# An attention loop regrouped: rounds of two score tiles, P·V in five bursts a head pair instead of nine

## The chip, the core and the metric

The kernel runs on one core of a Trainium2 chip. The metric is the device time of one execution in microseconds. The engines named below are TensorE (PE, its weight loads listed apart as PEld), VectorE (DVE), ScalarE (ACT), GpSimd (POOL) and the queue that issues the DMAs (SP).

## The reference

Attention over 2 batches and 8 heads, 1152 positions, head dimension 64, with the queries averaged in pairs (576 query rows), then a gated sum of four two-layer experts on the 1152 x 512 result, all in float32:

```python
q_pool = q.reshape(B, H, S // 2, 2, D).mean(axis=3)
scores = scale * np.matmul(q_pool, k.transpose(0, 1, 3, 2))
attn = np.exp(scores - np.max(scores, axis=-1, keepdims=True))
attn = attn / (np.sum(attn, axis=-1, keepdims=True) + 1e-09)
x = np.matmul(attn, v)            # then to (1152, 512)
for e in range(E):
    h = np.maximum(x @ w1[e], 0.0)
    out += p[:, e:e + 1] * (h @ w2[e])
```

## The kernel before

The attention stage goes over 8 pairs of heads (`n`). A pair has nine score tiles `i` of 128 query rows by 1152 keys: tiles 0 to 7 alternate between the two heads, tile 8 holds the last 64 rows of both. The 72 tiles are numbered through as `g = 9n + i`. A tile goes through these steps:

- `S_chunk` (L240): six matmuls (nine for tile 8) of 384 columns into the score tile `spt`, three banks of PSUM. The pool `ps_s` has one such buffer.
- `neg_scores` (L253): one DVE instruction takes all of `spt`, scales it, finds the row minimum `mn` and writes `sx`, of which there are three (`g % 3`).
- `exps` (L258): one ACT activation over `sx` in place, with the row sums into `sums`.
- `T_chunk` (L263): three transposes of 128 x 128 into a PSUM tile `pt`, three chunks a tile; the copy of chunk 1 into `aT` is on DVE, those of chunks 0 and 2 are on ACT.
- `PV_part` (L284): P·V from `aT` and `vn` into `po`, group 0 for tiles 0 to 3 (256 columns) and group 1 for tiles 4 to 8 (320 columns). Each of nine key blocks `kt` is a matmul for either head, 64 output columns wide, and the trace lists it as two instructions: four `L293` a key block. What is issued in one go is called a burst here.
- `diag_sums`, `spread_sums`, `finish` (L299 to L333): the reciprocal of the row sums (DVE, then POOL into `dg`), spread by four small matmuls into `rb`, and the division when a group is complete.

In between `prep_q` and `prep_k` transpose the next pair's queries and keys (three and five pieces), which POOL has split before (`split_pool`, `add_q`); SP moves their halves into place (`stack_k` into `kab`, the DMAs at L210 into `q2`).

The pool `ps_t` has four PSUM buffers under one tag: every `T_chunk`, every piece of `prep_q` and `prep_k` and every `spread_sums` takes one, in the order of the program, and the buffer comes free when its copy out has read it. `ps_o` has one buffer for `po`. Nothing is reordered: the kernel is built with a manual schedule, and each engine runs its instructions in the order in which the program emits them.

One round of the loop handles one tile, in the order of `ORDER`: `T0 prep T1 exp T2 P S bx`. So PE transposes tile g, prepares a piece for the next pair, does a burst of two or so key blocks, and makes the scores of tile g + 2; ACT's exponential of tile g + 1 stands between the copies of tile g. The matmuls of the first expert chunk are cut into 32 units: `fill(2)` puts two into each of the last two rounds, `fill(4)` four ahead of the last `spread_sums` and `PV_part`, and `fill(32)` the rest behind them. The expert stage follows (L461 on).

Of the kernel before, what the change touches and what calls it, by code (L numbers as in the profile page):

```python
# [17 lines left out]
def attention_moe_kernel(ctx, tc, q, k, v, probs, w1, w2, out):  # L18
    nc = tc.nc
# [3 lines left out]
    P = 128  # L23
# [89 lines left out]
    with ExitStack() as actx:  # L113
# [62 lines left out]
        def split_pool(dst, src):  # L176
            for h in range(2):
                split_rows(dst[:, h], src[:, h])
# [179 lines left out]
        for c in range(3):  # L358
            S_chunk(1, c)
        neg_scores(1)  # L360
        prep_q(0, 2)
        load_q(1)
        load_kv(kn, k, 1)
        add_q(nc.gpsimd)
# [5 lines left out]
        PVCUT = {0: (1, -1, 0, 3), 1: (1, -1, 3, 5), 2: (1, -1, 5, 7), 3: (1, -1, 7, 9),  # L370
                 4: (0, 0, 0, 2), 5: (0, 0, 2, 4), 6: (0, 0, 4, 6), 7: (0, 0, 6, 8), 8: (0, 0, 8, 9)}
        STAGES = {0: [(stack_k, 0, 0)], 1: [(stack_k, 0, 1)], 3: [(diag_sums, 0, 0)], 8: [(diag_sums, 0, 1)]}
        SPREAD = {6: (0, 0), 1: (-1, 1)}
        PREP = [None, ("q", 0), ("k", 0), ("k", 1), ("k", 2), ("q", 2), ("k", 3), ("k", 4), None]

        def pv_part(g):
            n, i = divmod(g, 9)
            grp, dn, k0, k1 = PVCUT[i]
            if 0 <= n + dn < NP:
                PV_part(n + dn, grp, k0, k1)  # L380

# [16 lines left out]
        ORDER = 'T0 prep T1 exp T2 P S bx'.split()  # L398
# [11 lines left out]
        for g in range(NTL):  # L410
            n, i = divmod(g, 9)
            if i == 4 and 0 < n and n + 1 < NP:
                load_kv(vn[(n + 1) % 2], v, n + 1)
            if i == (6 if n else 7) and n + 2 < NP:
                add_q(nc.gpsimd)
            if i == 0 and 0 < n and n + 1 < NP:
                split_pool(khl, kn)
            if i == 2 and 0 < n and n + 2 < NP:
                load_q(n + 2)
                load_kv(kn, k, n + 2)  # L420
            for step in ORDER:
                if step[0] == "T":
                    T_chunk(g, int(step[1]))
                elif step == "prep" and n + 1 < NP:
                    what = PREP[i]
                    if what:
                        (prep_q if what[0] == "q" else prep_k)(n + 1, what[1])
                elif step == "exp" and g + 1 < NTL:
                    exps(g + 1)
                elif step == "P":  # L430
                    pv_part(g)
                    if i in SPREAD and n + SPREAD[i][0] >= 0:
                        spread_sums(n + SPREAD[i][0], SPREAD[i][1])
                elif step == "S" and g + 2 < NTL:
                    for c in range(3):
                        S_chunk(g + 2, c)
                    neg_scores(g + 2)
                elif step == "bx":
                    for fn, dn, *args in STAGES.get(i, []):
                        fn(n + dn, *args)  # L440
            if (n, i) == (NP - 2, 0):
                load_weights(0)
            if (n, i) == (NP - 2, 7):
                load_weights(1)
                for kt in range(4):
                    split_weights(wslot[0], raw_piece(0, kt), kt)
            if (n, i) == (NP - 1, 2):
                load_weights(2)
            if (n, i) == (NP - 1, 7):
                for kt in range(4):  # L450
                    split_weights(wslot[1], raw_piece(1, kt), kt)
                load_weights(3)
            if g >= NTL - 2:
                fill(2)
# [101 lines left out]
```

## Time and profile before

| | us |
|---|---|
| median of 3 runs | 687.33 (686.88 to 687.66) |
| the profiled execution | 686.85 |
| its span in the trace | 685.1 |
| attention loop from the scores of tile 2 to the last `spread_sums` | 14.29 to 280.14 |
| PE busy in the span | 677.1 (99%) |

The execution's own time is 1.75 us above its span. A busy PE is not a PE at its peak: matmul ends in the trace are modelled and overlap, so the starts of the weight loads are what the order of the work is read from.

### The profile page before, as it was taken

Reading aid. Unit: us, or ns where it says so; the run is one execution under the profiler, and the core shown is the slowest. Engines: PE = TensorE matmul, PEld = TensorE weight load, DVE = VectorE, ACT = ScalarE, POOL = GpSimd, SP = SyncE. Lnnn points to the kernel's source line nnn. Section 1 sums busy time; section 2 is a strip of 40 time slices with the busy share of each in tenths; the row PEclk is TensorE's granted clock in tenths of the full one; section 3 lists DMA queues with packets and bytes.
Section 4 is the critical chain, followed back from the end, with each engine's and each line's share of the span. In section 5 each row is a group of like instructions: output and inputs, shape, how many; then the busy total and the mean of one; then the engine's idle time right before and its main releaser. Section 6 shows DMA issues by size and latency. Waiting matters only on the chain.

```text
span 685.1 us, 9897 instructions
## 1 busy us (share of the span) xinstructions
PE 677.1 (99%) x3986; PEld 576.2 (84%) x3986; DVE 248.1 (36%) x453; ACT 239.0 (35%) x473; POOL 201.9 (29%) x243
## 2 busy tenths in 40 slices
PE   7999999999999999999999999999999999999998
PEld 6777777777777777799989898989898989898987
DVE  5756565655656555321212121212121212121211
ACT  5867676767676666321111010101010202020200
POOL 4232323232323515392260080350170430310000
PEclk9999999999999999999999999999999999999999
DMA  7726262626252841031030030030040000001012
GB/s 241 168 52 184 54 181 59 179 61 174 64 172 54 235 131 51 12 123 61 1 124 1 0 95 30 29 94 1 0 124 1 32 30 1 0 1 32 15 43 52
DMA packets 26446, 50.75 MB, mean 74 GB/s; under 512 B 2464, under 2 KB 9888, under 8 KB 26400
## 3 DMA queue, kind: packets, MB, share of 16 engines
q1 hardware_dynamic: 26400, 50.12, 26.1%
q8 instruction: 32, 0.52, 0.3%
q14 instruction: 14, 0.11, 0.0%
HBM read 30.97 MB, written 2.36 MB: 49 GB/s over the span
## 4 chain that ended last, share of the span: by engine, by line
PE 91%; POOL 2%; ACT 2%; DVE 2%; issue 1%; DMA 1%; SPq 0%; POOLq 0%; DVEq 0%; ACTq 0%
PE p L504 29%; PE p L93 27%; PE spt L251 11%; PE po L293 11%; PE pt L268 9%; PE p1t L93 2%; ACT sx L260 2%; DVE sx L254 2%; PE pk L224 1%; PE pr L316 1%; DMA kn<-in_k_dram 1%; POOL q2all L102 1%; PE pq L198 0%; POOL q2all L99 0%; POOL dg L305 0%
## 5 line engine op out<-in xcount | busy, mean ns | idle before, releaser
L93 PE MATMUL p<-xh,wslot 128*128 128x384 f32 x640 | 166.7, 339 | 0.0
L254 DVE TENSOR_SCALAR_CACHE_REDUCE sx<-spt 128x1152 f32<-128x1152 f32 x72 | 97.7, 1357 | 101.8 <-PE spt L251 101.3
L93 PEld LDWEIGHTS p<-xh,wslot 128*128 128x128 f32 x640 | 116.7, 188 | 0.4
L93 PE MATMUL p<-xl,wslot 128*128 128x384 f32 x320 | 108.3, 338 | 0.0
L260 ACT ACTIVATE sx<-sx,mn 128x1152 f32<-128x1152 f32 x72 | 90.5, 1257 | 28.6 <-DVE sx L254 24.9
L268 PE MATMUL pt<-ident,sx 128*128 128x128 f32 x648 | 91.2, 275 | 0.9 <-ACT sx L260 0.4
L280 ACT ACTIVATE aT<-pt 128x384 f32<-128x384 f32 x144 | 69.6, 483 | 50.2 <-PE pt L268 49.9
L251 PEld LDWEIGHTS spt<-k,q2all 128*128 128x128 f32 x384 | 64.0, 188 | 27.4 <-DVE aT L278 9.7
L251 PE MATMUL spt<-k,q2all 128*128 128x384 f32 x384 | 84.8, 355 | 0.8 <-DVE sx L254 0.4
L293 PE MATMUL po<-aT,vn 128*64 128x320 f32 (+1 forms) x576 | 85.0, 418 | 0.0
L268 PEld LDWEIGHTS pt<-ident,sx 128*128 128x128 f32 x648 | 74.2, 141 | 6.5 <-ACT sx L260 4.5
L95 ACT ACTIVATE hb<-p 128x384 fp32r<-128x384 f32 x48 | 23.6, 491 | 160.0 <-PE p L93 160.0
L504 PE MATMUL p<-wslot,hb 128*128 128x512 f32 (+1 forms) x348 | 75.8, 375 | 0.0
L504 PEld LDWEIGHTS p<-wslot,hb 128*128 128x128 f32 x348 | 62.2, 188 | 11.7
L509 DVE SCALAR_TENSOR_TENSOR acc<-p,pw,acc 128x512 f32<-128x512 f32 (+1 forms) x28 | 20.5, 732 | 124.1 <-PE p L504 124.1
L333 POOL TENSOR_TENSOR xl<-xs,xh 128x256 fp32r<-128x256 f32 (+2 forms) x20 | 13.4, 677 | 165.0 <-ACT xh L332 165.0
L93 PEld LDWEIGHTS p<-xl,wslot 128*128 128x128 f32 x320 | 60.0, 188 | 0.4
L95 ACT ACTIVATE k<-p 128x384 fp32r<-128x384 f32 x30 | 14.7, 492 | 130.6 <-PE p L93 130.6
L293 PEld LDWEIGHTS po<-aT,vn 128*64 128x64 f32 x576 | 35.3, 136 | 27.1 <-issue 11.4
L99 POOL TENSOR_SCALAR wslot<-stg 128x512 fp32r<-128x512 f32 x12 | 7.5, 624 | 162.3 <-PE p L93 84.7
L96 DVE SCALAR_TENSOR_TENSOR hb<-p,hb 128x384 fp32r<-128x384 f32 x48 | 26.7, 557 | 76.7 <-ACT hb L95 76.7
L504 PE MATMUL p<-wslot,k 128*128 128x512 f32 x168 | 51.9, 390 | 0.0
(102 smaller groups left out, 770.1 us busy)
## 6 DMA issues: line engine op xcount, KB each, us to landing
kab<-k SPq DMA_DIRECT2D x32, 288.0 KB, 4.7
q2all<-q2all SPq DMA_DIRECT2D x28, 256.0 KB, 4.9
vn<-in_v_dram SPq DMA_DIRECT2D x8, 576.0 KB, 6.9
kn<-in_moe_w_dram SPq DMA_DIRECT2D x8, 512.0 KB, 3.7
qn<-in_moe_w_dram SPq DMA_DIRECT2D x8, 512.0 KB, 3.7
stg<-in_moe_w_dram SPq DMA_DIRECT2D x8, 512.0 KB, 3.5
qs<-in_moe_w_dram SPq DMA_DIRECT2D x8, 512.0 KB, 3.6
qn<-in_q_dram SPq DMA_DIRECT2D x7, 576.0 KB, 6.3
```

The lines of the kernel that those rows point to most:

```text
L93: nc.tensor.matmul(pt, w[:, a, kt, fs], x[:, kt, cols], start=(j == 0), stop=(j == last))
L95: nc.scalar.activation(hh[ft], pt, AF.Relu)
L96: nc.vector.scalar_tensor_tensor(hl[ft], pt, 0.0, hh[ft].bitcast(F32), ALU.max, ALU.subtract)
L251: nc.tensor.matmul(spt[g][:, c, :NC], w, x, start=(j == 0), stop=(j == len(ops) - 1))
L254: nc.vector.tensor_scalar(sx[g % 3].rearrange("p (c x) -> p c x", c=3), spt.pop(g)[:, :, :NC], -INV, None, ALU.mult, ALU.min, accum_out=mn ...
L260: nc.scalar.activation(sx[g % 3], sx[g % 3], AF.Exp, bias=mn[g % 3], scale=-1.0, accum_out=sums[n % 2][:, i:i + 1])
L268: nc.tensor.transpose(pt[:, j, :], sx[g % 3][:, kt * P:(kt + 1) * P], ident)
L280: nc.scalar.activation(dst, src, AF.Copy)
L293: nc.tensor.matmul(po[h * HALF:(h + 1) * HALF, :w], vn[n % 2][:, h, kt, :], aT[grp][:, h, kt, :], start=(kt == 0), stop=(kt == KT - 1))
L333: nc.gpsimd.tensor_tensor(xl[:, hp, c], x[:, s0:s0 + w], xh[:, hp, c].bitcast(F32), ALU.subtract)
L504: nc.tensor.matmul(pc, h[ft][:, ts_], where[e, 2, ft // 4][:, a, ft % 4, c0:c1], start=(m == 0), stop=(m == len(ops) - 1))
L509: nc.vector.scalar_tensor_tensor(ac, pc, pw[:, tt, e:e + 1], ac, ALU.mult, ALU.add)
```

## The change

The loop goes in rounds of two tiles (`i` = 0, 2, 4, 6) and a last round of one (`i` = 8). A round emits: the transposes of tile g, the exponential of tile g + 2, the transposes of tile g + 1, up to two pieces of preparation for the next pair, the scores of tile g + 3, one burst of P·V, the exponential of tile g + 3, and the scores of tile g + 4. The round of tile 8 has its transposes, a burst and the scores of tile g + 3. P·V goes in five bursts of 5 and 4 key blocks (group 1 of the pair before) and 3, 3 and 3 (group 0), where there were nine. `stack_k` and `split_pool` move to the round of tile 8 of the pair before, the pieces of preparation to rounds 0, 2, 4 and 6, the loads and `diag_sums` by one to three tiles; the scores of tile 2 and the exponential of tile 1 move ahead of the loop. In the last pair `fill(4)` stands where scores are missing.

```diff
@@ -358,26 +358,37 @@
         for c in range(3):
             S_chunk(1, c)
         neg_scores(1)
+        exps(1)
         prep_q(0, 2)
+        for c in range(3):
+            S_chunk(2, c)
+        neg_scores(2)
         load_q(1)
         load_kv(kn, k, 1)
+        for h in range(2):
+            stack_k(0, h)
         add_q(nc.gpsimd)
         split_pool(khl, kn)
         load_kv(vn[1], v, 1)
         load_q(2)
         load_kv(kn, k, 2)
 
-        PVCUT = {0: (1, -1, 0, 3), 1: (1, -1, 3, 5), 2: (1, -1, 5, 7), 3: (1, -1, 7, 9),
-                 4: (0, 0, 0, 2), 5: (0, 0, 2, 4), 6: (0, 0, 4, 6), 7: (0, 0, 6, 8), 8: (0, 0, 8, 9)}
-        STAGES = {0: [(stack_k, 0, 0)], 1: [(stack_k, 0, 1)], 3: [(diag_sums, 0, 0)], 8: [(diag_sums, 0, 1)]}
-        SPREAD = {6: (0, 0), 1: (-1, 1)}
-        PREP = [None, ("q", 0), ("k", 0), ("k", 1), ("k", 2), ("q", 2), ("k", 3), ("k", 4), None]
-
-        def pv_part(g):
-            n, i = divmod(g, 9)
+        PVCUT = {0: (1, -1, 0, 5), 2: (1, -1, 5, 9), 4: (0, 0, 0, 3), 6: (0, 0, 3, 6), 8: (0, 0, 6, 9)}
+        SPREAD = {6: (0, 0), 0: (-1, 1)}
+        PREP = {0: [("q", 0), ("q", 2)], 2: [("k", 0), ("k", 1)], 4: [("k", 2), ("k", 3)], 6: [("k", 4)]}
+
+        def pv_part(n, i):
             grp, dn, k0, k1 = PVCUT[i]
             if 0 <= n + dn < NP:
                 PV_part(n + dn, grp, k0, k1)
+            if i in SPREAD and n + SPREAD[i][0] >= 0:
+                spread_sums(n + SPREAD[i][0], SPREAD[i][1])
+
+        def scores(g):
+            if g < NTL:
+                for c in range(3):
+                    S_chunk(g, c)
+                neg_scores(g)
 
         for hh in range(2):
             nc.sync.dma_start(
@@ -395,7 +406,6 @@
                     nc.vector.tensor_copy(pw[sl, 5 * b:5 * b + 4, :], pr[sl, 9 * b + a:9 * b + 8:2, :])
                 nc.vector.tensor_copy(pw[sl, 4, :], pr[sl, 9 * a + 8, :])
 
-        ORDER = 'T0 prep T1 exp T2 P S bx'.split()
         tail = []
         units = [(ft, kt) for ft in range(NFT) for kt in range(NKT)]
 
@@ -407,51 +417,62 @@
                         tail.append(ps_t.tile([P, NC], F32, tag="t", name="p1t"))
                     mm1_ft(0, 0, ft, tail[-1], kt)
 
-        for g in range(NTL):
-            n, i = divmod(g, 9)
-            if i == 4 and 0 < n and n + 1 < NP:
-                load_kv(vn[(n + 1) % 2], v, n + 1)
-            if i == (6 if n else 7) and n + 2 < NP:
-                add_q(nc.gpsimd)
-            if i == 0 and 0 < n and n + 1 < NP:
-                split_pool(khl, kn)
+        for n, i in [(n, i) for n in range(NP) for i in range(0, 9, 2)]:
+            g = 9 * n + i
+            last = n == NP - 1
             if i == 2 and 0 < n and n + 2 < NP:
                 load_q(n + 2)
                 load_kv(kn, k, n + 2)
-            for step in ORDER:
-                if step[0] == "T":
-                    T_chunk(g, int(step[1]))
-                elif step == "prep" and n + 1 < NP:
-                    what = PREP[i]
-                    if what:
-                        (prep_q if what[0] == "q" else prep_k)(n + 1, what[1])
-                elif step == "exp" and g + 1 < NTL:
-                    exps(g + 1)
-                elif step == "P":
-                    pv_part(g)
-                    if i in SPREAD and n + SPREAD[i][0] >= 0:
-                        spread_sums(n + SPREAD[i][0], SPREAD[i][1])
-                elif step == "S" and g + 2 < NTL:
-                    for c in range(3):
-                        S_chunk(g + 2, c)
-                    neg_scores(g + 2)
-                elif step == "bx":
-                    for fn, dn, *args in STAGES.get(i, []):
-                        fn(n + dn, *args)
+            if i == 4:
+                if 0 < n and n + 1 < NP:
+                    load_kv(vn[(n + 1) % 2], v, n + 1)
+                diag_sums(n, 0)
+            if i == 6 and n + 2 < NP:
+                add_q(nc.gpsimd)
+            if i == 8:
+                diag_sums(n, 1)
+                if n + 1 < NP:
+                    for h in range(2):
+                        stack_k(n + 1, h)
+                if n + 2 < NP:
+                    split_pool(khl, kn)
+            for c in range(3):
+                T_chunk(g, c)
+            if g + 2 < NTL:
+                exps(g + 2)
+            if i < 8:
+                for c in range(3):
+                    T_chunk(g + 1, c)
+            if not last:
+                for kind, c in PREP.get(i, []):
+                    (prep_q if kind == "q" else prep_k)(n + 1, c)
+            if i < 8:
+                scores(g + 3)
+                if last and i == 6:
+                    fill(4)
+                pv_part(n, i)
+                if g + 3 < NTL:
+                    exps(g + 3)
+                scores(g + 4)
+                if last and i == 6:
+                    fill(4)
+            else:
+                if last:
+                    fill(4)
+                pv_part(n, i)
+                scores(g + 3)
             if (n, i) == (NP - 2, 0):
                 load_weights(0)
-            if (n, i) == (NP - 2, 7):
+            if (n, i) == (NP - 2, 6):
                 load_weights(1)
                 for kt in range(4):
                     split_weights(wslot[0], raw_piece(0, kt), kt)
             if (n, i) == (NP - 1, 2):
                 load_weights(2)
-            if (n, i) == (NP - 1, 7):
+            if (n, i) == (NP - 1, 6):
                 for kt in range(4):
                     split_weights(wslot[1], raw_piece(1, kt), kt)
                 load_weights(3)
-            if g >= NTL - 2:
-                fill(2)
         fill(4)
         spread_sums(NP - 1, 1)
         PV_part(NP - 1, 1, 0, KT)
```

## Rows read from the trace of the kernel before

**Rows 1.** The head of the page: the span, and busy time, share of the span and instructions of each engine.

```profile
span 685.1 us, 9897 instructions
...
PE 677.1 (99%) x3986; PEld 576.2 (84%) x3986; DVE 248.1 (36%) x453; ACT 239.0 (35%) x473; POOL 201.9 (29%) x243
```

**Rows 2.** Busy time of each engine by stage: the stretch in us, its length, busy time and (x) instructions of PE, PEld, DVE, ACT and POOL, granted clock of PE as a share of 2.4 GHz, DMA share and GB/s. The edges are starts of the scores of tile 2: of pair 0, pair 1 and pair 7, then the last `spread_sums`.

```profile
...
14.29:45.13 30.84, 30.21 (x214) 23.61 (x214) 20.65 (x40) 23.83 (x47) 8.84 (x11) 1.00 0.58 140
45.13:248.82 203.69, 203.37 (x1448) 153.72 (x1446) 121.54 (x228) 141.75 (x279) 68.09 (x87) 1.00 0.49 131
248.82:280.14 31.32, 31.08 (x211) 24.05 (x209) 15.38 (x29) 18.96 (x38) 12.83 (x18) 1.00 0.12 39
280.14:685.10 404.96, 401.64 (x2056) 365.53 (x2056) 82.59 (x143) 47.49 (x98) 106.44 (x114) 1.00 0.12 38
```

**Rows 3.** Weight loads of PE in order of time through one round of a middle pair: start, length, line, names, shape and count, and in brackets the idle time before the load and what ended it. Scores, transposes of chunk 0, a piece of `prep_k`, transposes of chunks 1 and 2, a burst, the next scores.

```profile
...
151.38 1.01 PEld L251 LDWEIGHTS spt<-k,q2all 128*128 128x128 f32 x6 [0.49 <-DVE aT L278]
152.38 0.42 PEld L268 LDWEIGHTS pt<-ident,sx 128*128 128x128 f32 x3
152.77 0.42 PEld L224 LDWEIGHTS pk<-identr,khl 128*128 128x128 f32 x4
153.14 0.64 PEld L268 LDWEIGHTS pt<-ident,sx 128*128 128x128 f32 x6
153.95 0.74 PEld L293 LDWEIGHTS po<-aT,vn 128*64 128x64 f32 x8 [0.17 <-issue]
155.18 1.00 PEld L251 LDWEIGHTS spt<-k,q2all 128*128 128x128 f32 x6 [0.49 <-issue]
...
```

**Rows 4.** Who waited for whom, for PEld: us in total, times, longest us.

```profile
...
PEld po L293 <- issue: 11.4, 68, 0.2
...
```

**Rows 5.** The same view as rows 3, other bursts and what follows them: 320 columns with a `spread_sums`, 256 columns, 320 columns with three key blocks.

```profile
...
149.61 0.74 PEld L293 LDWEIGHTS po<-aT,vn 128*64 128x64 f32 x8 [0.17 <-issue]
150.47 0.41 PEld L316 LDWEIGHTS pr<-dg,ones 128*64 128x64 f32 x4
...
161.50 0.63 PEld L293 LDWEIGHTS po<-aT,vn 128*64 128x64 f32 x8 [0.17 <-issue]
162.51 1.00 PEld L251 LDWEIGHTS spt<-k,q2all 128*128 128x128 f32 x6 [0.39 <-DVE aT L278]
...
179.15 1.27 PEld L293 LDWEIGHTS po<-aT,vn 128*64 128x64 f32 x12 [0.17 <-issue]
180.91 1.00 PEld L251 LDWEIGHTS spt<-k,q2all 128*128 128x128 f32 x6 [0.49 <-issue]
...
```

**Rows 6.** DVE and ACT in order of time, in the round of rows 3: `neg_scores`, the copy of chunk 1, the exponential, the copy of chunk 2.

```profile
...
152.75 1.36 DVE L254 TENSOR_SCALAR_CACHE_REDUCE sx<-spt 128x1152 f32<-128x1152 f32 x1 [1.90 <-PE spt L251]
154.04 0.08 DVE L254 DVE_READ_ACCUMULATOR sx<-spt 128x1 f32 x1
154.04 0.55 DVE L278 COPY aT<-pt 128x384 f32<-128x384 f32 x1
...
154.22 1.25 ACT L260 ACTIVATE sx<-sx,mn 128x1152 f32<-128x1152 f32 x1 [0.15 <-DVE sx L254]
...
155.47 0.47 ACT L280 ACTIVATE aT<-pt 128x384 f32<-128x384 f32 x1
```

**Rows 7.** Weight loads, then DVE and ACT, at the end of that pair: a round with a burst of one key block, and the start of the next round.

```profile
...
173.77 0.99 PEld L251 LDWEIGHTS spt<-k,q2all 128*128 128x128 f32 x6 [0.39 <-DVE aT L278]
...
176.00 0.20 PEld L293 LDWEIGHTS po<-aT,vn 128*64 128x64 f32 x4 [0.17 <-issue]
176.63 1.01 PEld L251 LDWEIGHTS spt<-k,q2all 128*128 128x128 f32 x6 [0.44 <-DVE sx L254]
178.02 0.96 PEld L268 LDWEIGHTS pt<-ident,sx 128*128 128x128 f32 x9 [0.37 <-ACT sx L260]
...
176.50 0.08 DVE L254 DVE_READ_ACCUMULATOR sx<-spt 128x1 f32 x1
...
177.78 0.18 ACT L260 ACTIVATION_READ_ACCUMULATOR sx<-sx,mn 128x1 f32 x1
```

**Rows 8.** The scores of tile 8 (weight loads) and their `neg_scores` (DVE).

```profile
...
169.86 1.52 PEld L251 LDWEIGHTS spt<-kab,q2all 128*128 128x128 f32 x9 [0.39 <-DVE aT L278]
...
171.74 1.36 DVE L254 TENSOR_SCALAR_CACHE_REDUCE sx<-spt 128x1152 f32<-128x1152 f32 x1 [2.08 <-PE spt L251]
```

**Rows 9.** Weight loads of the six `fill` units ahead of the last `spread_sums`, the first and the last of 18, and that `spread_sums`.

```profile
...
276.46 0.19 PEld L93 LDWEIGHTS p1t<-xh,wslot 128*128 128x128 f32 x1 [0.38 <-issue]
...
279.39 0.19 PEld L93 LDWEIGHTS p1t<-xh,wslot 128*128 128x128 f32 x1
280.14 0.20 PEld L316 LDWEIGHTS pr<-dg,ones 128*64 128x64 f32 x4 [0.56 <-POOL dg L309]
```

**Rows 10.** POOL, the first and the last of the four instructions of a `split_pool`; and SP, the DMAs of a `stack_k`, their issue.

```profile
...
147.62 0.68 POOL L173 TENSOR_SCALAR khl<-kn 128x576 fp32r<-128x576 f32 x1
...
150.52 1.41 POOL L174 TENSOR_TENSOR khl<-kn,khl 128x576 fp32r<-128x576 f32 x1
...
154.09 2.48 SPq L214 DMA_DIRECT2D kab<-k  x2
...
```

**Rows 11.** `finish` in a middle pair: the division (DVE) and the copy into `xh` (ACT).

```profile
...
159.17 0.49 DVE L323 TENSOR_TENSOR xs<-po,rb 128x320 f32<-128x320 f32 x1 [0.20 <-PE po L293]
...
159.69 0.47 ACT L332 ACTIVATE xh<-xs 128x320 fp32r<-128x320 f32 x1
```

## The prediction, before the changed kernel was run

> **What bounds the kernel now.** I read the head of the page first: PE is busy for 677.1 of 685.1 us [rows 1], DVE, ACT and POOL for about a third. So a microsecond is won or lost only on PE. The stages come next [rows 2]: the change touches the loop from 14.29 to 280.14 us; the 404.96 us behind it are expert matmuls and stay. Pairs 1 to 6 take 203.69 / 6 = 33.95 us each, pair 0 takes 30.84 and the last stretch 31.32. The granted clock is 1.00 (2.4 GHz) in all of them; the bubbles below are under 0.7 us each, and I count nothing for the clock.
>
> The order of PE's weight loads shows what a burst costs [rows 3]. The transposes' last load ends at 153.78, the burst's first starts at 153.95: 0.17 us, which 68 of the 69 bursts pay (pair 0 has five, one stands behind the loop) [rows 4]. Eight instructions of 320 columns take 1.23 us until the next scores start, twelve take 1.76 [rows 3, 5]: 0.135 each and some 0.15 once. So a burst removed is worth about 0.17 + 0.15 = 0.32 us. The Trainium skill says the same of the cause (TensorEngine Tiling (Array Packing), Key Properties: changing the tiling mode drains TensorE); by that rule alone the change gains, and the sum it gives is the first rival below.
>
> Then the engines that feed PE. From the first weight load of a score tile (time 0 from here on), its `neg_scores` starts on DVE at 1.37, the next DVE instruction (the copy of chunk 1) at 2.66 and ends at 3.21; the exponential starts on ACT at 2.84 and the next ACT instruction at 4.09, a copy that ends at 4.56 [rows 3, 6]. Both copies had been ready long before: they stand behind the score tile's work in their queues. Today that costs nothing, because with at most four pieces a round each `ps_t` buffer is asked for again only a round later. PE goes on about 0.06 us after the end of what it waits for (176.58 to 176.63, 177.96 to 178.02), and two score tiles cannot follow each other by less than 2.86 us, since `spt` is single (173.77 to 176.63) [rows 7].
>
> **What the change removes.** Four bursts a pair, 4 x 0.32 = 1.28 us, and one 0.37 wait of a round's first transpose for its exponential [rows 7], since exponentials are now early. Four of the five bursts left follow scores, not transposes. No row shows that switch: at least the 0.17 of a transpose; at most the 0.49 that loads wait behind a burst [rows 3]. The last score matmul is longer than a transpose by some 0.11 (0.17 a load against 0.64 / 6), so I take 0.28, nearer the first.
>
> **What it adds: two waits for a PSUM buffer.** A round now takes six chunks and up to two pieces in a row from four buffers. I read the pool as handing them out in turn, so a piece waits for the copy of the piece four before it.
> Free flow first: scores 0.98, three transposes 0.42, fifteen more at 0.107: chunk 2 of tile g + 1 would start at 2.68 and end at 3.00.
> *Wait 1.* That chunk takes the buffer of chunk 1 of tile g. Its copy is on DVE behind `neg_scores` of tile g + 2, whose scores stand right ahead of these transposes. It ends at 3.21, PE goes on at 3.27: 0.59 lost, in every round but that of tile 8. Chunk 2 ends at 3.59.
> *Wait 2.* The second piece of preparation takes the buffer of chunk 0 of tile g + 1. Its copy is on ACT behind the exponential of tile g + 2, which needs `neg_scores` of that tile, and ends at 4.56: the piece starts at 4.62, where PE would be at 3.59 + 0.38 = 3.97. Another 0.65 lost in rounds 0, 2 and 4.
> The cause is the same: the scores of tile g + 2 stand directly ahead of the transposes of tile g, and their DVE and ACT work is queued ahead of the copies out. Behind those copies wait the buffers; behind the buffers, PE.
> The Trainium skill speaks against the change here: Perfetto Trace Analysis, Optimization Strategy, reads a gap that repeats on the engine that should be saturated as a possible lack of PSUM for the next tile. The rows before show no such gap; by the sum below the changed kernel has it.
>
> **A middle pair, from the scores of tile 2 to those of the next pair.** Bursts to the next scores: 320 columns, 12 instructions 1.76, each four more 0.54 (1.76 - 1.23); 256 columns, 8 take 1.01, each four more 0.43 [rows 5]. A `spread_sums` counts as four: eight and its four take 1.77 [rows 3, 5].
> - Round 0: second piece (one transpose, 0.11) ends at 4.73; scores 0.98; switch 0.28; 20 + 4 instructions 1.76 + 3 x 0.54 = 3.38. Together 9.37.
> - Round 2: piece ends at 4.62 + 0.40 = 5.02; 0.98 + 0.28; 16 instructions 2.30. 8.58.
> - Round 4: 5.02; by the burst 0.98 + 0.28 + 1.44 later, but `spt` is free only 2.86 after: 7.88.
> - Round 6: behind tile 8, whose nine loads take 1.52 and whose `neg_scores` starts at 1.88 [rows 8], all is 0.52 later: chunk 2 ends at 4.11; piece of two 0.22; 0.98 + 0.28; 12 + 4 instructions 1.87. 7.46.
> - Round 8: burst starts at 2.23 [rows 7] and takes 1.44: 3.67.
> Sum 36.96, against 33.95: +3.01 a pair, +18.1 for six.
> **Pair 0** has no group 1 before it, so rounds 0 and 2 have no burst and are bound by `spt`: 4.73 + 2.86 = 7.59, and 7.88; then 7.88, 7.46, 3.67: 34.48 against 30.84, +3.6.
> **The last stretch** has no preparation, so wait 1 alone: 3.59 + 0.98 + 0.28 + 3.38 = 8.23; 7.15; 3.59 + 2.86 = 6.45; then from tile 8's scores to the last `spread_sums` 4.11 + four groups of four units + two bursts 1.87 and 1.44 + transposes 1.08 + three switches 0.84. A unit is 0.52 (18 loads from 276.46 to 279.58) [rows 9], so 8.32 for the four groups: 17.66. Together 39.49, against 31.32; but 16 units are then done, not 8, and 8 x 0.52 = 4.16 come off behind: +4.0. (The cuts are at the same instruction, so work moved between stretches shows in both; only the total counts.)
> Total 18.1 + 3.6 + 4.0 = +25.7 us: the span to 710.8, the profiled execution to 712.6; the median is 0.48 above the profiled execution, so 687.33 + 25.7 = **713.0 us**.
>
> **Edits costed at nothing.** `split_pool` goes to POOL a round earlier and lasts 4.3 us (147.62 to 151.93) [rows 10]; its reader, the first key piece, comes in round 2, over 10 us later. `stack_k` issues the same DMAs on SP in 2.48 us [rows 10]; `kab` is read by tile 8's scores in round 4, some 20 us later, and the DMAs at L210 behind it in round 0 have until round 6. If one were late, PE would stand still at those scores, one for one. `diag_sums` comes earlier than its readers need it. `finish` is new ahead of an exponential on ACT in round 2: division 0.49 and copy 0.47 after the burst, then 1.25 [rows 6, 11], about 2.1 after the next scores start, when the transposes want it at 2.06: at most 0.3 a pair, inside the range.
>
> **Rivals.**
> *The change does what it says, with no wait* (buffers not taken in turn, or copies not held up). For it: the drains are real [rows 3, 4]. Against: the order of the queues [rows 6] and four buffers for eight pieces. Free flow gives rounds of 8.15, 7.36, 6.66, 6.87 and 3.67 = 32.71, -1.24 a pair, -7.4 for six; pair 0 6.37 + 6.66 + 6.66 + 6.87 + 3.67 = 30.23, -0.6; the last stretch 39.49 less 4 x 0.59, +1.6. In all -6.4: 680.9 us. It decides on one point: whether the copy of chunk 1 is out by 2.6 after the scores start, not 3.21.
> *Wait 1 alone* (the second piece finds a free buffer): 32.71 + 4 x 0.59 = 35.07 a pair, +6.7; pair 0 32.59, +1.8; last +4.0: +12.5, 699.8 us. Against: the exponential stands in ACT's queue ahead of that copy.
> *The switch behind scores costs 0.49*: 0.21 more in 3 rounds of each middle pair and a few others, +5; with 0.17 it is -3. This bounds the sum: 710 to 718.
> *A draw*: waits of about a third of the size pay back the drains.
>
> **How the numbers follow.** The two waits as summed 0.75, wait 1 alone 0.10, no wait 0.11, a draw 0.04. The sum's own range is 706 to 722: the switch, a slow restart of PE after each of some 50 waits (0.1 each, +5), `finish`. The 80% range reaches down to the second rival: 697 to 722. 0.2% (1.4 us) is about what a measurement can tell from no change: faster 0.11, same 0.04, slower 0.85.
>
> **What would show it.** In the trace after: 39 bursts in place of 69; PEld idle ahead of `pt` for about 0.6 us in rounds 0 to 6, ended by the DVE copy L278; idle ahead of `pk` or `pq` for about 0.65, ended by the ACT copy L280; a pair of about 37 us with DVE and ACT no busier; scores of tile 8 about 2.86 behind those of tile 7. If transposes run 18 in a row without a gap, the prediction is wrong and the first rival right.

## The result, and the profile of the changed kernel

The changed kernel takes 697.59 us (696.6 to 698.29, four runs), against 687.27 for the kernel before on the same chip: a ratio of 1.0149, 95% interval 1.0131 to 1.0167, or +10.3 us. The forecast was +25.7. The span of the profiled execution grows by 10.2 us, 685.1 to 695.3, and its head answers to [rows 1]:

```profile
span 695.3 us, 9839 instructions
...
PE 680.8 (98%) x3986; PEld 581.6 (84%) x3986; DVE 249.1 (36%) x453; ACT 235.0 (34%) x473; POOL 202.0 (29%) x243
```

The same work on every engine, and a PE still busy nearly throughout. Busy time by stage, cut at the same instructions and in the columns of [rows 2], with the start as the first row:

```profile
0.00:14.17 14.17, 10.22 (x53) 8.33 (x53) 8.16 (x13) 6.05 (x12) 5.72 (x15) 1.00 0.68 212
14.17:50.22 36.05, 31.35 (x202) 26.39 (x202) 20.12 (x38) 23.25 (x46) 7.40 (x9) 0.91 0.64 145
50.22:256.06 205.84, 203.70 (x1448) 155.63 (x1446) 122.04 (x228) 138.11 (x279) 67.99 (x87) 1.00 0.46 124
256.06:294.58 38.52, 38.12 (x256) 29.99 (x254) 17.33 (x33) 20.82 (x43) 14.25 (x20) 1.00 0.14 45
294.58:695.30 400.72, 397.40 (x2033) 361.30 (x2032) 81.49 (x141) 46.78 (x96) 106.61 (x114) 1.00 0.12 38
```

| stage | before | after | difference | forecast |
|---|---|---|---|---|
| start | 14.29 | 14.17 | -0.1 | 0 |
| pair 0 | 30.84 | 36.05 | +5.2 | +3.6 |
| pairs 1 to 6 | 203.69 | 205.84 | +2.2 | +18.1 |
| last stretch and the rest | 436.28 | 439.24 | +3.0 | +4.0 |

So the whole miss lies in the six middle pairs, 34.31 us each instead of 36.96. Who waited for whom, for PEld (us in total, times, longest):

```profile
PEld spt L251 <- DVE sx L254: 13.7, 18, 3.1
PEld po L293 <- issue: 9.0, 38, 0.3
PEld spt L251 <- issue: 6.9, 14, 0.5
PEld pt L268 <- ACT aT L280: 4.0, 24, 0.2
PEld pt L268 <- ACT sx L260: 3.3, 7, 0.5
...
PEld pk L224 <- DVE aT L278: 1.1, 3, 0.5
```

38 waits ahead of a burst, not 68 [rows 4]: the bursts went from 69 to 39 as meant. The long waits of `pt` for the DVE copy L278, which the prediction asked for, are not in the list; in their place stand 24 of 0.17 us on ACT's copy L280, and three of a piece (`pk`) for L278. One middle pair, weight loads in order of time, to be held against [rows 3, 5, 7]:

```profile
153.20 1.01 PEld L251 LDWEIGHTS spt<-k,q2all 128*128 128x128 f32 x6 [0.38 <-DVE aT L278]
...
161.71 1.00 PEld L251 LDWEIGHTS spt<-k,q2all 128*128 128x128 f32 x6 [0.49 <-issue]
162.69 1.73 PEld L268 LDWEIGHTS pt<-ident,sx 128*128 128x128 f32 x15
164.59 0.31 PEld L268 LDWEIGHTS pt<-ident,sx 128*128 128x128 f32 x3 [0.17 <-ACT aT L280]
165.01 0.79 PEld L224 LDWEIGHTS pk<-identr,khl 128*128 128x128 f32 x8
165.75 1.00 PEld L251 LDWEIGHTS spt<-k,q2all 128*128 128x128 f32 x6
166.99 1.81 PEld L293 LDWEIGHTS po<-aT,vn 128*64 128x64 f32 x16 [0.25 <-issue]
169.30 1.00 PEld L251 LDWEIGHTS spt<-k,q2all 128*128 128x128 f32 x6 [0.49 <-issue]
170.29 1.08 PEld L268 LDWEIGHTS pt<-ident,sx 128*128 128x128 f32 x9
171.80 1.07 PEld L268 LDWEIGHTS pt<-ident,sx 128*128 128x128 f32 x9 [0.43 <-ACT sx L260]
172.91 0.86 PEld L224 LDWEIGHTS pk<-identr,khl 128*128 128x128 f32 x8
173.72 0.99 PEld L251 LDWEIGHTS spt<-k,q2all 128*128 128x128 f32 x6
...
176.58 1.54 PEld L251 LDWEIGHTS spt<-kab,q2all 128*128 128x128 f32 x9 [0.56 <-DVE sx L254]
...
183.74 1.00 PEld L251 LDWEIGHTS spt<-k,q2all 128*128 128x128 f32 x6 [0.39 <-DVE sx L254]
...
187.43 1.01 PEld L251 LDWEIGHTS spt<-k,q2all 128*128 128x128 f32 x6 [0.39 <-DVE aT L278]
```

The rounds begin at 153.20, 161.71, 169.30, 176.58 and 183.74. Against the prediction's sums, and its sums with no wait at all:

| round | forecast | no wait | measured |
|---|---|---|---|
| 0 | 9.37 | 8.15 | 8.51 |
| 2 | 8.58 | 7.36 | 7.59 |
| 4 | 7.88 | 6.66 | 7.28 |
| 6 | 7.46 | 6.87 | 7.16 |
| 8 | 3.67 | 3.67 | 3.69 |
| pair | 36.96 | 32.71 | 34.23 |

In round 2, fifteen transposes run in a row; chunk 2 of tile g + 1 waits 0.17 and starts 2.88 after the scores' first load (161.71), not 3.27; the first piece starts at 3.30 where free flow has it at 3.00; the second follows it without a gap. On DVE in that round, then on ACT, as in [rows 6]:

```profile
163.06 1.36 DVE L254 TENSOR_SCALAR_CACHE_REDUCE sx<-spt 128x1152 f32<-128x1152 f32 x1 [1.94 <-PE spt L251]
...
164.34 1.01 DVE L278 COPY aT<-pt 128x384 f32<-128x384 f32 x2
```

```profile
163.43 1.11 ACT L280 ACTIVATE aT<-pt 128x384 f32<-128x384 f32 x2
164.52 1.26 ACT L260 ACTIVATE sx<-sx,mn 128x1152 f32<-128x1152 f32 x1
```

DVE's copy of chunk 1 stands behind `neg_scores`, as forecast. It starts at 164.34; with the 0.55 of [rows 6] it is out at 164.89, 3.18 after the scores, and the piece starts 0.12 later. So the copy is as late as forecast, but the piece takes its buffer, and the piece is wanted 0.3 later than chunk 2. Chunk 2 takes the buffer that ACT's second copy gives back at 164.54. DVE's second copy is out at 165.35, about when the first piece is done (165.01 + 0.40), so the second piece waits for nothing.

Which buffer a piece takes needn't be inferred from waits alone. The program that the kernel is built into has a bank for every tile, fixed before it runs, and it says the same without exception: in all 32 rounds 0, 2, 4 and 6, chunk 2 of tile g + 1 gets the bank of chunk 2 of tile g; the first piece gets that of chunk 1 of tile g (28 of 28), the second that of chunk 1 of tile g + 1 (21 of 21). So chunk 2 follows a copy of ACT, and both pieces follow copies of DVE.

### The profile page after: what moved, and what is told of

It is laid out like the page before. It is cut to its first block, busy times and chain, and to the rows that moved or that the text cites. A ratio compares the mean times of both kernels' runs of the same rounds, so it can differ in the third digit from the quotient of the medians.

```text
span 695.3 us, 9839 instructions
## 1 busy us (share of the span) xinstructions
PE 680.8 (98%) x3986; PEld 581.6 (84%) x3986; DVE 249.1 (36%) x453; ACT 235.0 (34%) x473; POOL 202.0 (29%) x243
## 4 chain that ended last, share of the span: by engine, by line
PE 93%; DVE 4%; ACT 2%; issue 1%; POOL 0%; DVEq 0%; POOLq 0%; ACTq 0%
PE p L525 28%; PE p L93 27%; PE spt L251 12%; PE pt L268 10%; PE po L293 9%; PE p1t L93 3%; DVE sx L254 2%; PE pk L224 2%; ACT sx L260 1%; PE pr L316 1%; PE pq L198 1%; PE warm L342 0%; ACT xh L332 0%; DVE xs L323 0%; ACT q2all L181 0%
## 5 line engine op out<-in xcount | busy, mean ns | idle before, releaser
L268 PE MATMUL pt<-ident,sx 128*128 128x128 f32 x648 | 85.1, 281 | 1.6 <-ACT sx L260 1.6
L293 PE MATMUL po<-aT,vn 128*64 128x320 f32 (+1 forms) x576 | 78.4, 412 | 0.0
L280 ACT ACTIVATE aT<-pt 128x384 f32<-128x384 f32 x144 | 65.7, 484 | 19.5 <-PE pt L268 18.5
L293 PEld LDWEIGHTS po<-aT,vn 128*64 128x64 f32 x576 | 38.0, 136 | 30.5 <-issue 9.0
L305 POOL TENSOR_TENSOR dg<-ident,rs 128x256 f32<-128x256 f32 x32 | 19.0, 615 | 102.5 <-DVE rs L303 99.5
```

What stands on the lines that cost most here:

```text
L268: nc.tensor.transpose(pt[:, j, :], sx[g % 3][:, kt * P:(kt + 1) * P], ident)
L280: nc.scalar.activation(dst, src, AF.Copy)
L293: nc.tensor.matmul(po[h * HALF:(h + 1) * HALF, :w], vn[n % 2][:, h, kt, :], aT[grp][:, h, kt, :], start=(kt == 0), stop=(kt == KT - 1))
L305: nc.gpsimd.tensor_tensor(dg[:, h, :256].rearrange("p (j q) -> p j q", j=2), ident.unsqueeze(1).to_broadcast([P, 2, P]), r[:, h:4:2].unsqu ...
```

## The experiments

The time before was 686.89 to 687.50 us beside them. Unless said otherwise a kernel is the changed one with one edit; it stood at 697.59.

| run | time, us | ratio to before, 95% interval |
|---|---|---|
| aturn | 717.27 | 1.0438 (1.0420 to 1.0455) |
| bturn | 688.33 | 1.0014 (1.0005 to 1.0023) |
| acopy2 | 701.69 | 1.0209 (1.0194 to 1.0224) |
| askip | 696.91 | 1.0142 (1.0123 to 1.0160) |
| aprep | 714.79 | 1.0403 (1.0387 to 1.0418) |
| aexp | 695.34 | 1.0118 (1.0101 to 1.0135) |
| asplit | 699.27 | 1.0173 (1.0155 to 1.0190) |
| awarm | 695.72 | 1.0120 (1.0105 to 1.0136) |
| b5 | 698.90 | 1.0167 (1.0152 to 1.0182) |
| b3 | 689.95 | 1.0041 (1.0028 to 1.0053) |
| acombo | 690.85 | 1.0052 (1.0039 to 1.0066) |
| b3late | 688.93 | 1.0030 (1.0018 to 1.0042) |

**Were the waits wrong, or only the buffer? (aturn, bturn.)** `ps_t` is replaced by four pools of one buffer, handed out in turn, in the changed kernel (aturn) and in the kernel before (bturn); nothing else differs.

```diff
+    def ps_tile(shape, dtype, name):
+        taken[0] += 1
+        return ps_t4.tile(shape, dtype, tag=f"t{taken[0] % 4}", name=name)
...
-            pt = ps_t.tile([P, 3, P], F32, tag="t", name="pt")
+            pt = ps_tile([P, 3, P], F32, "pt")
```

> The changed kernel with the four PSUM buffers of the transposes handed out strictly in turn (four pools of one buffer, taken in a circle), nothing else. The prediction had reckoned with this: chunk 2 of tile g + 1 then waits for DVE's copy of chunk 1 of tile g (0.59 us in rounds 0 to 6), the second piece of preparation for ACT's copy of chunk 0 of tile g + 1 (0.65 in rounds 0, 2 and 4). If these two waits are sized right and only the order of the buffers was wrong, the time is about 710 to 715 us, with PEld waits of pt on DVE aT and of pk or pq on ACT aT of that size. If the waits themselves were sized wrong, it stays within 5 us of the changed kernel's 697.6.

> The kernel before with its four PSUM buffers handed out strictly in turn in the same way: the control for the run above. With at most four pieces a round each buffer is asked for a round later, so every theory expects no change beyond 0.2%, 687.3 us; a rise would mean that the form of the pool costs something by itself.

aturn, weight loads of PE in round 2 of a middle pair (its lines are numbered 6 higher), then two lines of its waits:

```profile
171.60 1.00 PEld L257 LDWEIGHTS spt<-k,q2all 128*128 128x128 f32 x6 [0.49 <-issue]
172.59 1.73 PEld L274 LDWEIGHTS pt<-ident,sx 128*128 128x128 f32 x15
174.84 0.31 PEld L274 LDWEIGHTS pt<-ident,sx 128*128 128x128 f32 x3 [0.53 <-DVE aT L284]
175.12 0.42 PEld L230 LDWEIGHTS pk<-identr,khl 128*128 128x128 f32 x4
176.19 0.39 PEld L230 LDWEIGHTS pk<-identr,khl 128*128 128x128 f32 x4 [0.64 <-ACT aT L286]
```

```profile
PEld pt L274 <- DVE aT L284: 17.7, 31, 1.2
...
PEld pk L230 <- ACT aT L286: 8.3, 14, 0.9
```

Chunk 2 starts at 3.24 (forecast 3.27), the second piece at 4.59 (forecast 4.62), and a pair takes 199.29 - 162.24 = 37.05 us (forecast 36.96). Its rounds take 9.36, 8.48, 8.08, 7.46 and 3.67 us, where the prediction's sums have 9.37, 8.58, 7.88, 7.46 and 3.67. Both waits are real, with their sizes, once buffers go in turn. The whole, 717.27, is above the 710 to 715 expected, mostly by pair 0, which takes 36.65 us (forecast 34.48). In the kernel before the order of buffers costs 0.14% (bturn, 0.05 to 0.23), and its middle pairs take 33.94 us with it and 33.95 without. So the step that failed is the reading of the pool. Perfetto Trace Analysis, Optimization Strategy, of the Trainium skill reads a repeating gap on the busiest engine as a possible want of PSUM: aturn has such gaps, 31 and 14 times, where the changed kernel, with the same four banks in another order, has 24 of 0.17 us. So the order of the buffers counts beside their number, and no run here has more of them.

**What holds the first piece? (acopy2, askip.)** acopy2 gives DVE the copy of chunk 2 instead of chunk 1; askip leaves out the copy of chunk 2 of tiles 0, 2, 4 and 6 in pairs 1 to 7.

```diff
-            if c == 1:
+            if c == 2:
                 nc.vector.tensor_copy(dst, src)
```
```diff
+            if c == 2 and n > 0 and i in (0, 2, 4, 6):
+                return
```

> The changed kernel with one digit changed in T_chunk: DVE copies chunk 2 of a tile and ACT chunks 0 and 1 (before: DVE chunk 1). Chunk 2 of tile g + 1 can then take the buffer of chunk 1 of tile g, which ACT has copied by 2.6 us after the scores started, when it is wanted at 2.68; now it waits for chunk 2's copy until 2.88 and loses 0.28 with the restart. If this wait is the larger part of what the order costs, about 30 x 0.28 = 8 us go, to 689 to 691 us. If a piece of preparation or ACT takes the wait over, it stays within 2 us of 697.6.

> The changed kernel without the copy of chunk 2 of the first tile of each round (tiles 0, 2, 4 and 6) in pairs 1 to 7; P.V reads what pair 0 left there. It shows what the wait for that buffer costs in all: PE does the same work, and the buffer is free when the transposes are done. If the 0.17 us wait and the slow restart behind it are what keeps the changed kernel from the gain of its fewer bursts, 28 x 0.28 = 8 us go, to 690 us. If the next buffer in line then makes PE wait, less than 3 us go.

Either was to gain 8 us if the wait for ACT's copy was what counts. acopy2 lost 4.1, outside both of its cases; askip gained 0.7, as in its second case. Even that isn't the wait: askip leaves pair 0 as it is, and in the profiles pair 0 alone is 0.7 shorter (35.31, at a granted clock of 0.95 instead of 0.91), while the middle pairs take 34.29 on average against 34.31. askip, round 2 of a middle pair, and the piece of round 6:

```profile
161.06 1.00 PEld L251 LDWEIGHTS spt<-k,q2all 128*128 128x128 f32 x6 [0.49 <-issue]
162.05 2.06 PEld L268 LDWEIGHTS pt<-ident,sx 128*128 128x128 f32 x18
164.37 0.80 PEld L224 LDWEIGHTS pk<-identr,khl 128*128 128x128 f32 x8 [0.26 <-issue]
...
179.82 0.22 PEld L224 LDWEIGHTS pk<-identr,khl 128*128 128x128 f32 x2 [0.29 <-DVE aT L280]
```

The wait of 0.17 is gone and eighteen transposes run in 2.06 without a gap, but the first piece still starts 3.31 after the scores, and the pair still takes 34.23 (186.79 - 152.56). The wait on ACT, the one that the list of waits names, was not the limit: DVE's copy behind `neg_scores` was, one step later. It starts at 163.70 and is out 0.55 later, 0.12 ahead of the piece, and in round 6 the view names it. No run takes this copy away, so that it is the limit is read from the rows. In acopy2 the first piece starts at the same 3.30, and the second now waits for DVE as well (with the piece of round 6 21 times, 7.3 us).

**Pieces between the two tiles (aprep).** The pieces of rounds 0, 2 and 4 go between the transposes of tile g and of tile g + 1.

```diff
                 exps(g + 2)
+            if not last and i < 6:
+                for kind, c in PREP.get(i, []):
+                    (prep_q if kind == "q" else prep_k)(n + 1, c)
...
-            if not last:
+            if not last and i == 6:
```

> The changed kernel with the preparation pieces of rounds 0, 2 and 4 issued between the transposes of tile g and those of tile g + 1, not behind both. In the changed kernel chunk 2 of tile g + 1 waits 0.17 us for ACT's copy of chunk 2 of tile g and loses about 0.28 with the restart. If the wait is for the buffer, the pieces now give the copies time: 0.28 x 3 a pair for seven pairs, about -5 us. If the wait only moves (to a piece, or to the exponential of tile g + 1), the time stays within 1 us or rises.

The 5 us of the first case did not come; the second did, and far more strongly: 17 us slower. Its longest waits:

```profile
PEld pt L268 <- ACT aT L280: 17.2, 23, 2.0
```

The copies of the pieces and of tile g + 1 now all stand behind the exponential on ACT, and chunks wait up to 2.0 us for them. The place of the exponential in ACT's queue is what wait 2 was about; here it comes true. Part of the 17 us is the clock: pairs 2, 4 and 5 take 37.9 to 38.0 us at a granted clock of 0.95 or 0.96, pairs 1, 3 and 6 36.4 to 36.7 at 1.00.

**The exponential behind `finish` (aexp).** The exponential of tile g + 3 goes ahead of the burst.

```diff
-                pv_part(n, i)
                 if g + 3 < NTL:
                     exps(g + 3)
+                pv_part(n, i)
```

> The changed kernel with one line moved: the exponential of tile g + 3 is issued ahead of the burst, so that on ACT it stands in front of the copies of finish and spread_sums. In the changed kernel's trace PEld waits 0.43 to 0.53 us for ACT sx in round 4 of each pair from 1 on, because finish of group 1 stands ahead of that exponential. If that is the cause these waits go and the time falls by about 3 us (to 694.5). If the exponential was held by something else (DVE, the scores) the time stays within 0.5 us.

2.25 us faster than the changed kernel. The seven waits of `pt` on ACT's exponential (3.3 us, 0.43 in round 4 above) are gone. Part comes back as a wait of 0.32 in the same round for DVE's copy, which stands there behind `diag_sums`. What the repair is worth is less than 2.25: a middle pair takes 34.12 us against 34.31, 1.1 for six, while 0.7 lies in pair 0 (35.35, again at 0.95), which never had this wait.

**One burst more (asplit).** The second piece goes into the middle of the burst, which gives 19 bursts more.

```diff
-                PV_part(n + dn, grp, k0, k1)
+                PV_part(n + dn, grp, k0, k0 + 2)
+                for kind, c in pieces[1:]:
+                    (prep_q if kind == "q" else prep_k)(n + 1, c)
+                PV_part(n + dn, grp, k0 + 2, k1)
...
```

> The changed kernel with the second piece of preparation of rounds 0, 2 and 4 issued in the middle of the burst instead of ahead of the scores: the same work, but 19 bursts more. By the drains read from the trace (0.25 ahead of a burst, 0.15 behind it, and a load that is no longer hidden) each is worth 0.4 us: +6 to +8 us, to 704. If a burst costs nothing by itself and the gain of fewer bursts was never there, the time stays within 1.5 us of 697.6.

Only +1.7, which fits neither case, and it is a sum: the six middle pairs lose 2.8 (34.77 on average against 34.31), and pair 0, where scores now come ahead of the second piece and the granted clock is 0.95, gains 1.8 (34.28). The scores that begin rounds 0, 2 and 4 of a middle pair, and tile 8's:

```profile
152.89 1.01 PEld L251 LDWEIGHTS spt<-k,q2all 128*128 128x128 f32 x6 [0.39 <-DVE aT L278]
...
161.66 1.00 PEld L251 LDWEIGHTS spt<-k,q2all 128*128 128x128 f32 x6 [0.49 <-issue]
...
169.48 0.99 PEld L251 LDWEIGHTS spt<-k,q2all 128*128 128x128 f32 x6 [0.49 <-DVE k L229]
...
176.73 1.52 PEld L251 LDWEIGHTS spt<-kab,q2all 128*128 128x128 f32 x9 [0.38 <-issue]
```

This pair takes 187.57 - 152.89 = 34.68 us, 0.45 more: 8.77 in round 0 and 7.82 in round 2, so 0.26 and 0.23 for a burst, and 7.25 in round 4, where it hides behind the wait for `spt`. So 0.32 for a burst was high by a quarter. TensorEngine Tiling (Array Packing), Key Properties, of the Trainium skill says that a change of tiling mode drains TensorE. The trace agrees: a gap of 0.25 or 0.26 stands ahead of each burst that follows scores.

**Pair 0 and its clock (awarm).** In the changed kernel's pair 0: weight loads of PE, then DVE, then busy time by stretches of 4 us, with the granted clock in the third column from the right:

```profile
14.17 1.78 PEld L251 LDWEIGHTS spt<-k,q2all 128*128 128x128 f32 x6 [1.65 <-DVE sx L254]
15.94 2.54 PEld L268 LDWEIGHTS pt<-ident,sx 128*128 128x128 f32 x15
...
23.62 1.11 PEld L251 LDWEIGHTS spt<-k,q2all 128*128 128x128 f32 x6 [3.13 <-DVE sx L254]
```

```profile
21.12 0.69 DVE L182 TENSOR_TENSOR q2all<-pq,q2all 128x512 fp32r<-128x512 f32 x1 [1.79 <-ACT q2all L181]
21.72 0.45 DVE L193 TENSOR_TENSOR q2all<-pq,q2all 64x64 fp32r<-64x64 f32 x2
22.20 1.36 DVE L254 TENSOR_SCALAR_CACHE_REDUCE sx<-spt 128x1152 f32<-128x1152 f32 x1
```

```profile
12.00:16.00 4.00, 2.65 (x11) 2.35 (x11) 1.49 (x3) 1.67 (x4) 1.69 (x2) 0.78 0.96 208
16.00:20.00 4.00, 4.00 (x28) 3.71 (x27) 2.71 (x6) 2.38 (x5) 2.08 (x3) 0.80 1.01 205
20.00:24.00 4.00, 1.19 (x7) 0.87 (x6) 2.41 (x5) 1.72 (x6) 2.06 (x3) 1.00 1.03 228
24.00:28.00 4.00, 4.00 (x21) 3.90 (x20) 1.84 (x3) 2.31 (x5) 0.00 (x0) 0.57 0.98 297
```

PE stands still 1.65 us ahead of the scores of tile 2 and 3.13 ahead of those of tile 4, and behind either the clock falls to the lower of its two levels (1.2 GHz) for a part of the stretches shown: 0.78 and 0.57 of 2.4 GHz on average, fifteen transposes in 2.54 instead of 1.73. The second stop has a cause of its own: `neg_scores` of tile 3 stands on DVE behind the query split of round 0, which waits 1.79 for ACT. awarm puts identity transposes into a PSUM bank that is idle then, 12 ahead of the scores of tile 2 and 16 in place of each burst that pair 0 lacks.

```diff
         prep_q(0, 2)
+        keep_warm(12)
...
+            elif n + dn < 0:
+                keep_warm(16)
```

> The changed kernel with transposes of the identity into the unused P.V bank put where pair 0 has no burst: 12 ahead of the loop's first scores and 16 in each of rounds 0 and 2. They change no result. Pair 0 took 36.05 us (30.84 before) at a granted clock of 0.91. If half of that is the clock, which fell after PE had stood still there, the clock in 14 to 50 us is 1.00 and the time falls by 2 to 4 us. If the waits for the single score buffer are all of it, the clock changes nothing that counts and the time stays within 1 us.

1.9 us faster, a little short of the 2 to 4. Pair 0 falls from 36.05 to 33.26 us (15.36 to 48.62), with transposes at full speed (fifteen in 1.73 in round 2); 1.2 of it is paid ahead, since the first twelve run at 0.57 and take 2.57. So the first fall wasn't prevented: half of the stretch from 12 to 13 us is at the lower level (0.75 on average), and the fillers start only at 12.80, with no stop above 1.53 ahead of them. What is gone is the second fall. How much of the 1.9 is the clock is open: of the four runs of the changed kernel the one with a mean granted clock of 0.998 took 696.6, those with 0.993 took 697.89 and 698.29; awarm's two runs with 0.998 took 695.7. The wait on DVE stays, at 1.19.

**The halves of the change (b5, b3).** b5 is the kernel before with the five bursts alone, b3 the kernel before with the scores three tiles ahead alone.

```diff
-        PVCUT = {0: (1, -1, 0, 3), 1: (1, -1, 3, 5), 2: (1, -1, 5, 7), 3: (1, -1, 7, 9),
-                 4: (0, 0, 0, 2), 5: (0, 0, 2, 4), 6: (0, 0, 4, 6), 7: (0, 0, 6, 8), 8: (0, 0, 8, 9)}
+        PVCUT = {0: (1, -1, 0, 5), 1: (1, -1, 5, 5), 2: (1, -1, 5, 9), 3: (1, -1, 9, 9),
+                 4: (0, 0, 0, 3), 5: (0, 0, 3, 3), 6: (0, 0, 3, 6), 7: (0, 0, 6, 6), 8: (0, 0, 6, 9)}
```
```diff
...
-                elif step == "S" and g + 2 < NTL:
+                elif step == "S" and g + 3 < NTL:
...
```

> The kernel before with nothing changed but the cuts of P.V: five bursts a pair (5, 4, 3, 3, 3 key blocks in rounds 0, 2, 4, 6, 8), the order of everything else as it was. If a burst removed is worth its drain and nothing else moves, 4 x 0.32 us a pair go, about -9 us on 687.3. If the single score buffer takes it back: a round without a burst has only 2.6 us of PE work from one score tile to the next and is held at 2.86, and the transposes behind it wait some 0.4 us for their exponential; worked out round by round that is about 36 us a pair, +10 to +15 us.

> The kernel before with one part of the change alone: the scores are made three tiles ahead, not two (those of tile 2 ahead of the loop); rounds of one tile and nine bursts stay. In the kernel before each pair loses 0.37 us where the transposes of a pair's first tile wait for their exponential, and 0.05 where scores wait for spt. If the scores' lead is what cures the first, about 0.4 us a pair go, -3 us, to 684, faster than both. If a lead without longer rounds only moves the wait to spt, the time stays within 0.2% of 687.3.

b5 loses 11.4 us, and a middle pair takes 179.91 - 144.61 = 35.30. A round without a burst is too short for the single score tile and its exponential:

```profile
PEld spt L251 <- DVE sx L254: 12.8, 24, 0.7
PEld pt L268 <- ACT sx L260: 12.6, 27, 1.2
```

b3's middle pairs do gain, 33.71 against 33.95, as the waits for exponentials go; the whole is 0.4% slower, a miss. Its start has the same stop as the changed kernel's (1.75 us ahead of the scores of tile 2, then nine transposes in 2.01 instead of 1.01), and the scores of tile 8 of pair 6, a tile earlier, wait 1.09 for a DMA into `kab`. The clock alone isn't its loss: the one of its five runs with a mean granted clock of 1.00 took 690.89, the longest.

**A better version? (acombo, b3late.)** acombo joins aexp and awarm, puts the query pieces of round 0 of pair 0 behind the scores, and cuts group 0 into 4, 3 and 2 key blocks. b3late is b3 from tile 6 on only.

```diff
+                if step == "T1" and g == 4:
+                    for c in range(3):
+                        S_chunk(6, c)
+                    neg_scores(6)
...
-                elif step == "S" and g + 2 < NTL:
+                elif step == "S" and g + (2 if g < 4 else 3) < NTL:
```

> The changed kernel with four repairs: the exponential of tile g + 3 ahead of the burst, transposes of the identity in pair 0 where there is no burst, the query pieces of the very first round behind its scores (they held neg_scores back on DVE), and group 0 cut 4, 3, 2. If the parts add up (-2.3 and -1.9 measured, -1.2 for neg_scores in the first round, -1 for the cut, since the scores of tile 8 no longer wait for spt), 691 us: still slower than before, because the wait for a PSUM buffer in each round stays. If the parts overlap, 693 to 694.

> The kernel before, with the scores three tiles ahead of the transposes only from tile 6 on: the start and tiles 0 to 3 stay as they were, the scores of tile 6 go between the chunks of tile 4, those of tile 7 behind its burst; bursts and all else as before. My theory: what the scores-ahead half of the change did wrong alone (689.95) lies in its start, where the third score tile waits for the single score buffer and the clock falls; the middle pairs gained 0.24 us each (33.71 against 33.95). Without that start there remain six or seven pairs by 0.24, -1.4 to -1.7, less some 0.3 for the two score tiles close together in tile 4: 685.8 us, ratio 0.998, with a mean granted clock of 1.00 in the first 45 us and a middle pair of 33.7. Rival: the loss lies elsewhere (in the last stretch, where fewer scores are left to stand between the transposes, or in the later copies of each round): then 688 to 690, whatever the start looks like.

acombo came out as expected, 6.7 us below the changed kernel: pair 0 takes 31.60 us (30.84 before), a middle pair 33.94 (135.76 / 4) against 33.95. With five bursts and the side costs mended the loop comes out even in its middle, no better. b3late missed by 3.1 us, inside the range of its rival, if not for the rival's reasons. Its middle pairs take 33.70, as expected, but tile 8's scores, a tile earlier, wait 1.05 in pair 0 (0.38 before; the view names DVE) and 0.48 more for the DMA into `kab`, and 0.97 for that DMA in pair 6, and the clock fell in the start all the same, though PE's order there is that of the kernel before (0.67 from 10 to 15 us, nine transposes in 1.93 instead of 1.01, the scores of tile 2 0.86 later). Together these are some 3 us against a gain of six times 0.25; the span grew by 1.9. That they explain it is read from the rows, not tried, and the clock's part is doubtful: the one of its six runs with a mean granted clock of 1.00 took 689.56, more than the median. No version beat the kernel before. b3late with `stack_k` a round earlier wasn't tried.

## Why the prediction was half right

- **The bound and the sign** held: PE sets the time, DVE and ACT are no busier, and waits for copies and the single score tile eat the saved drains.
- **What a burst is worth** was a little high: 0.32 forecast, some 0.25 measured in the changed kernel (asplit). The switch from scores to a burst was right: it starts 1.24 to 1.30 after the scores (166.99 - 165.75, 158.33 - 157.03), 0.98 + 0.28 forecast, with a gap of 0.25 or 0.26 in the rows.
- **Wait 1** had the right engine, the right cause and the right moment (the copy is out at 3.18; forecast 3.21), but it hits the piece behind chunk 2: 0.3 a round instead of 0.59.
- **Wait 2** did not come, because the second piece takes the other buffer that DVE empties, not ACT's. This was the larger share of the miss: 0.65 in three rounds, 1.95 us of each pair. Free flow (32.71), 0.3 in four rounds and the 0.43 of `finish` give 34.34, against 34.31 measured on average.
- **The step that failed** is one sentence: "I read the pool as handing them out in turn". The banks and the waits show another order, and aturn makes the sentence true and gives the forecast's own pair (37.05 against 36.96). It follows that chunk 2 waited 0.17 where 0.59 was put, and the second piece not at all where 0.65 was put.
- **Pair 0** was summed by `spt` alone and put at +3.6; it took +5.2. "I count nothing for the clock" was wrong there (awarm got 1.9 us back net, not all of it by the clock), and `neg_scores` of tile 3 behind the query split was not seen.
- **`finish`** ahead of the exponential cost 0.43, in round 4 where its transposes come, and was put at "at most 0.3 a pair"; with its exponential ahead (aexp) a middle pair is 0.19 shorter, as another wait takes its place.
- **The last stretch** was near: +3.0 against +4.0, with 0.17 for wait 1 there too, not 0.59.
- **The rivals.** The measured time lies between "wait 1 alone" (699.8) and no wait (680.9), nearest the former, whose mechanism it is at half the size; it was given 0.10. The stated range reached down to 697 for this rival's sake alone; the sum's own range, 706 to 722, misses the time, so the wider one holds 697.59, and barely, by that rival and not by the sum. The condition of the first rival, the copy of chunk 1 out by 2.6, was the wrong test: the copy was not out by then, and chunk 2 didn't need it. So was the sign of eighteen transposes without a gap: askip has them, and the pair is no faster.

## What to carry to other kernels

Where a forecast hangs on which buffer of a pool comes next, the order is an unknown with a price: here two orders lie 20 us apart. The built program holds the bank of every tile, so the order can be read before anything is summed; where it can't be read, sum more than one. A queue that delays a copy is read well from the trace; whom it delays depends on who takes that buffer. Fewer and longer bursts save here only about 0.25 us each on PE, and they bunch what DVE and ACT must do into the time between them, so the single-buffered tile and the copies behind the longest instruction decide.

## What the runs showed of the hardware

- The clock fell behind stops of 1.65 and 3.13 us in pair 0 (granted 0.78 and 0.57 in the stretches shown), while the waits of under 0.7 us in the middle pairs left it at 1.00.
- The fall isn't tied to the order of instructions alone. The kernel before, bturn, b5, b3late and awarm have the same order on PE up to 12.5 us, with one stop of 1.53 or 1.54 that ends at 10.1 or 10.2. From 12 to 14 us the profiles of the first two show 1.00, those of b5 and b3late 0.50, that of awarm 0.63. In b3late the scores of tile 2 start 0.86 later.
- The same holds in a steady loop: aprep's middle pairs have waits of up to 2.0 us, and the clock fell in three of the six, which took 37.9 to 38.0 us, and not in the others, which took 36.4 to 36.7.
- A wait of PE that disappears may have hidden another: without the 0.17 on ACT's copy (askip) a gap of 0.26 stands in its place, in round 2 put down to nothing but the issue, in round 6 to DVE's copy (0.29), and the piece starts at the same moment after the scores (3.31 against 3.30).
